# One attention-and-FFN block: head quads of the last two query tiles regrouped, VectorE's share of the exponentials chosen by new rules, and the first stage reordered

## The chip, the cores and the metric

The kernel runs on one core of a Trainium2 chip. The metric is the device time of one execution in microseconds (us), as the median of several runs. A NeuronCore has five engines with a queue each: TensorE (PE, matrix products into PSUM), ScalarE (ACT, here the exponentials), VectorE (DVE, elementwise work), GpSimd (POOL) and SyncE (SP, which issues nearly all DMAs here). PSUM has eight banks of 128 x 512 fp32 values.

## The reference, cut to what matters

```python
mod = (silu(c) @ w_mod)                      # six rows of 512: sa, ca, ga, sb, cb, gb
h = layernorm(x) * (1 + ca) + sa             # x is 2048 tokens x 512
qkv = h @ wqkv                               # 32 heads of 16
p = softmax(q k^T / 4)                       # 32 heads x 2048 x 2048
x = x + ga * ((p @ v) @ wo)
h = layernorm(x) * (1 + cb) + sb
x = x + gb * ((gelu(h @ w_gate) * (h @ w_up)) @ w_down)   # F = 1792
```

## The kernel before, in words

**Scores in banks.** The queries are cut into six sets (`SETS`, line 31): three of 512 tokens, one of 256, and the last two tiles of 128 tokens each (sets 4 and 5 in the code's numbers). Heads go in eight quads of four. A *unit* is a quad with a set; the first `QS = 5` quads (line 34) of the last two tiles are taken together, as units of 256 queries with the sets (4, 5), and the other three quads separately, first all of set 4, then all of set 5 (lines 1199 to 1201). A unit is cut into *rounds*: one round has four banks, one per head, each of 128 keys on the partitions by 512 columns (one key tile by 512 queries, two by 256 or four by 128). A unit of 512, 256 or 128 queries has 16, 8 or 4 rounds. There are 2048 banks in all, in one fixed sequence; `pos` is the place in it, and `ends[k]` the place where set k is complete: 512, 1024, 1536, 1792, 2000 and 2048. So the separate units lie at 1952 to 2000 (set 4) and 2000 to 2048 (set 5).

**The main loop** (`stream`, line 1192) puts three banks of scores (`CH`) into one half of a six-bank PSUM tile `ps_sc`, ACT takes their exponential in one instruction into a ring `E` of twelve banks, and PE multiplies them with the values into `ps_pv`, whose 17th row per head is the softmax's sum. While one half is on ACT, PE fills the other.

**Rounds on VectorE.** In some steps DVE takes one of the three banks instead of ACT: it writes an integer that, read as bf16, is close to the exponential (line 1394), and in four such steps a whole round. Four shifted copies of that round (`shift_task`, line 1472, `mreg<-dreg` or `mreg<-mreg` in the trace) with four scaled sets of values then average the error out; PE multiplies all five. Only rounds over the last four key tiles qualify: four of a 512-unit's rounds, two of a 256-unit's, one of a 128-unit's. A round is given (lines 1358 to 1374) when DVE is free within 700 ns by the planner's own clock, fewer than eight DVE steps wait (`BACK`), one of three buffers is free, the round lies less than 96 and at least `AHEAD = 24` banks ahead of `pos`, and, after `ends[2]`, the side work's credit is below `CREDIT = 1024`.

**Side work.** All other PE work (projections, output projection `side_wo`, FFN `side_ffn`) is a list of generators (`plan`, line 1118), taken strictly in order, with a bank `ps_mi` of its own. Each entry has a start and a due place in the sequence; `credit` grows by the columns left over the banks left, and PE does side work where credit and slack allow (lines 1350 and 1421). A generator that has to wait for something yields None (`until`, line 771), and `next_side` then returns None. The FFN of set 3 is due at `ends[4] - 20`, and what follows, the end of set 4, starts at `ends[4] - 16` (lines 1134 to 1143): the sums of its quads 6 and 7 (`near_end`, line 935: a product with `self32` spreads the sums, a reciprocal, and a product into `onorm`), its output projection, and then in `either` three things at once: the first two chunks of its FFN (`side_ffn(k, EARLY)`), the output projection of set 5 without its last quad (`wo_last`) and the rest of set 4's FFN (`tail_rest`). The last two wait for "last", when all scores are in PSUM. Quad 6 of set 5 gets its sums by a `near_end` behind the two chunks (line 1058). For the other quads the sums go through DRAM by small DMAs (`unit_end`, line 1494).

**DVE's and ACT's small work** is a list of tasks; `step` (line 1085) takes the first one that is ready, by `urgency` (line 1075). `tail` (line 1536) runs what is left when the last scores have been multiplied: sums of quad 7 of set 5, its output projection, LayerNorm, transposes, and the FFN of that tile, all in a row (`tail_end`, `tail_last`). All orders are settled when the program is built, by a cost model in the kernel's text; on the chip each engine runs its queue in order, with semaphores.

**First stage** (`prologue`, line 499). LayerNorm of the first four token tiles on DVE (tile 1 on ACT), two groups of 16 one-column products for the modulation (`mod_cols`, 4 to 7 and then 0 to 3, each from a 512 KB piece of `w_mod`), an addition `modA` on DVE, 16 transposes, `modulate`, the first projections and the first scores. `warm_up(n)` is n products of 128 x 512 on zeros.

Of the kernel before, what the change touches and what calls it, by code (L numbers as in the profile page):

```python
# [6 lines left out]
ALU = mybir.AluOpType  # L7
# [6 lines left out]
P = 128  # L14
# [16 lines left out]
SETS = ((0, 512), (512, 512), (1024, 512), (1536, 256), (1792, 128), (1920, 128))  # L31
OCOL = (0, 0, 0, 0, 256, 384)
BCOL = (0, 0, 0, 0, 0, 128)
QS = 5
CH = 3
SC = 2 * CH
NSL = 12
# [3 lines left out]
NK = 3  # L41
CREDIT = 1024
NS = 4
AHEAD = 24
FLOW = 3
URGENT = 9
LATE = 2
# [1 line left out]
BACK = 8  # L49
# [369 lines left out]
class _Kernel(_Recorder):  # L419
# [79 lines left out]
    def prologue(self):  # L499
# [46 lines left out]
        self.stt(self.sc_bf[:, :], self.tcol[:, :], 1.0, self.scp[:, 0, 0:NDC], ALU.add, ALU.mult)  # L546
        self.ln_stat(2)
        self.ln_stat(3)
        self.warm_up(7)
        self.mod_cols(self.scp[:, 1, 0:8], 0, range(4, 8))  # L550
        self.warm_up(3)
        self.mod_cols(self.scp[:, 1, 0:8], 0, range(4))
        self.warm_up(2)
        self.ln_rstd(0, 4)
        nb = self.nwt[:, 0:4]
        self.stt(nb, self.mv[:, 0:4, 0], -1.0, self.rstd[:, 0:4], ALU.mult, ALU.mult)
        for t in range(4):
            dst = self.tb1[:, 0, t, :]
            if t != 1:
                self.ln_norm(t, dst)  # L560
                if t == 0:
                    self.tt(dve, self.modA[:, :], self.modA[:, :], self.scp[:, 1, 0:8], ALU.add)
            else:
                self.act(dst, self.xs[:, t, :], ACT.Identity, bias=nb[:, t:t + 1], scale=self.rstd[:, t:t + 1])
        qb = [self.scp[:, 0, 0:256], self.scp[:, 1, 0:256]]
        kb = self.pv[:, 0:256]
        pts = []
# [202 lines left out]

    def until(self, key):
        while not self.dry and key not in self.have:
            yield None

    def side_first(self):
# [193 lines left out]
    def side_ffn(self, gi, part=None):  # L969

        q0, W = SETS[gi]
        n = W // P
        tiles = [q0 // P + i for i in range(n)]
        mi = self.mi[:, :]
        c0 = BCOL[gi]
        prod = self.prodT if W == 512 else self.prodL
        flow = gi < FLOW
        kpb = 512 // W
        chunks = []
        width = max(2, kpb)  # L980
        for a in range(0, NFC, width):
            chunks.append(range(a, min(NFC, a + width)))

        def load(x, ci):
            if flow and ci < len(chunks):
                v = (self.B_w_gate, self.B_w_up)[x].rearrange("(a p) n -> p a n", p=P)
                self.dma("sp", self.wst[x][ci % 2], v[:, :, 2 * P * ci:2 * P * ci + 2 * P], "st%d%d" % (x, ci % 2))

        def load_down(i):
            if flow:  # L990
                v = self.B_w_down.rearrange("(f p) n -> p f n", p=P)
                self.dma("sp", self.wdst[i], v[:, 2 * i:2 * i + 2, :], "sd%d" % i)

        yield from self.until(("ln2", gi))
        if flow:
            load(0, 0)
            load(1, 0)
        else:
            yield from self.until("weights")
        for h in range(2):  # L1000
            yield from self.side_t(lambda t: self.normed(gi, t), n, h,
                                   lambda dc: self.t2T[:, dc, c0:c0 + W], self.modB)

        def up(x, ci, sub):
            for s, fc in enumerate(sub):
                for dci in range(NDC):
                    if flow:
                        lhs = self.wst[x][ci % 2][:, dci, P * (fc % 2):P * (fc % 2) + P]
                    else:
                        lhs = self.up_w((self.wg, self.wu)[x], fc, dci)  # L1010
                    yield W, lambda s=s, lhs=lhs, dci=dci: self.mm(
                        mi[:, W * s:W * s + W], lhs, self.t2T[:, dci, c0:c0 + W], start=(dci == 0), stop=(dci == NDC - 1), whole=W == P)

        def G(ci):
            fcs = chunks[ci]
            m = len(fcs)
            g, w = self.gw[:, ci % 2, 0, 0:m * W], self.gw[:, ci % 2, 1, 0:m * W]
            load(0, ci + 1)
            for b0 in range(0, m, kpb):
                sub = fcs[b0:b0 + kpb]  # L1020
                yield from up(0, ci, sub)
                self.copy("dve", g[:, W * b0:W * (b0 + len(sub))], mi[:, 0:W * len(sub)])
                if b0 + kpb >= m and not self.dry:
                    self.task([lambda: self.tt("dve", w, g, g, ALU.mult),
                               lambda: self.ts("dve", w, w, GELU_C, 1.0, ALU.mult, ALU.add),
                               lambda: self.tt("dve", w, w, g, ALU.mult),
                               ("act", lambda: self.act(w, w, ACT.Tanh, scale=TANH_C0))], ("gelu", gi, ci))
                yield END

        def U(ci):  # L1030
            fcs = chunks[ci]
            m = len(fcs)
            g, w = self.gw[:, ci % 2, 0, 0:m * W], self.gw[:, ci % 2, 1, 0:m * W]
            yield from self.until(("gelu", gi, ci))
            load(1, ci + 1)
            for b0 in range(0, m, kpb):
                sub = fcs[b0:b0 + kpb]
                k = len(sub)
                yield from up(1, ci, sub)
                self.stt(w[:, W * b0:W * (b0 + k)], w[:, W * b0:W * (b0 + k)], 1.0, mi[:, 0:W * k], ALU.add, ALU.mult)  # L1040
                if b0 + kpb >= m:
                    self.tt("dve", prod[:, fcs[0]:fcs[0] + m, c0:c0 + W], w.rearrange("p (k n) -> p k n", k=m),
                            g.rearrange("p (k n) -> p k n", k=m), ALU.mult)
                yield END
        nch = len(chunks) if part is None else part
        for i in range(3):
            load_down(i)
        for ci in range(nch + 1):
            if ci < nch:
                yield from G(ci)  # L1050
                if ci >= nch - 2:
                    load_down(3 + ci - nch + 2)
            if ci >= 1:
                yield from U(ci - 1)
                if ci >= nch - 1:
                    load_down(5 + ci - nch + 1)
        if part is not None:
            yield from self.near_end(gi + 1, 6, self.mi[:, 0:P])
            if not self.dry:
                self.done(("part", gi))  # L1060
            return
        for i in range(n):
            for fc in range(NFC):
                yield 512, lambda i=i, fc=fc: self.mm(
                    mi, prod[:, fc, P * i:P * i + P], (self.wdst if flow else self.wd)[fc // 2][:, fc % 2, :], start=(fc == 0), stop=(fc == NFC - 1))
            self.down_fin(mi, tiles[i])
            yield END
        self.done(("ffn", gi))
# [5 lines left out]

    def urgency(self, tk):

        if tk[1] is not None and tk[1][0] == "shift" and self.plain[tk[1][1]] <= LATE:
            return -2
        if tk[1] is None or tk[1][0] in ("st2", "ln2", "den"):
            return -1  # L1080
        if tk[1] is None or tk[1][0] != "shift":
            return 1
        return 0 if self.plain[tk[1][1]] <= URGENT else 2
# [108 lines left out]
    def stream(self):  # L1192
        self.split = True
        self.tasks = []
        self.live = {}
        self.have = {("k", 0, 0), ("q", 0, 0), ("v", 0, 0)}
        self.credit = 0
        self.open = False
        units = [((k,), qd) + SETS[k] for k in range(4) for qd in range(8)]
# [3 lines left out]
        rounds = []  # L1203
# [15 lines left out]
        for u in units[2:]:  # L1219
# [3 lines left out]
            for r in plain[:m] + list(range(len(plain), n)) + plain[m:]:  # L1223
                add(u, r)
        nseq = len(seq)
        self.work = self.plan(ends, nsplit)
        self.slot = {}
        vec = set()
# [17 lines left out]
        quad = None  # L1246
# [84 lines left out]
        while cg <= group[units[-1]]:  # L1331
# [16 lines left out]
            if tq is not None and tq <= t + 30:  # L1348
# [7 lines left out]
                    continue  # L1356
                g = None
                if len(mem) == CH and "modB" in self.have and self.free["dve"] < t + 700:
                    while quad is None and cand and rounds[cand[0]][2] < pos + AHEAD:
                        cand.pop(0)  # L1360
                    overdue = {x[1][1] for x in self.tasks if x[1] is not None and x[1][0] == "shift" and self.plain[x[1][1]] <= LATE}
                    if quad is not None:
                        if not overdue - {quad["rnd"][0]}:
                            g = quad["rnd"][2] + quad["j"]
                    elif (not overdue and cand and self.quad_free and (pos < ends[2] or self.credit < CREDIT) and rounds[cand[0]][2] < pos + 96 and self.backlog() < BACK
                          and ("vs", rounds[cand[0]][0][1] // 2) in self.have
                          and all(k in self.have for k in self.keys(seq[rounds[cand[0]][2]]))):
                        rnd = rounds[cand.pop(0)]
                        quad = {"rnd": rnd, "j": 0, "k": self.quad_free.pop(0), "ready": [], "n": NS + 1, "slots": {}}
                        left[rnd[0]] += NS  # L1370
                        self.plain[rnd[0]] -= 1
                        g = rnd[2]
                        vec.update(range(g, g + 4))
                        mem, after = take(CH)
# [369 lines left out]
```

## Time and profile before

| what | before |
|---|---|
| median of 3 runs | 864.12 us (861.3 to 864.8) |
| the profiled execution, its own time | 864.73 us |
| its span, first to last instruction | 862.6 us (2.1 us lie around it) |
| busy: PE, DVE, ACT | 801.2, 694.8, 833.8 us |
| ACT's first and last exponential | starts 14.87, ends 841.08 us |
| ACT instructions of 1536 and 1024 columns on `E<-ps_sc` | 376 and 316 |
| DVE instructions that take a bank (192 `dreg<-ps_sc`, 96 `mreg<-ps_sc`) | 288, so 72 rounds |

Times in the profile are us from the span's start. A line of the timeline has start, duration, engine, source line, operation, `out<-in`, count, and in brackets the engine's idle time before it and what ended it. PE is engine work, PEld weight loads, a `q` after an engine's name its sequencer. Durations overlap for pipelined instructions.

### The profile page before, as it was taken

What the parts mean: (1) busy time and instruction counts of PE and PEld (TensorE: products, weight loads), DVE (VectorE), ACT (ScalarE), POOL (GpSimd) and SP (SyncE); (2) the same over time, 40 slices, a digit from 0 to 9 for tenths busy, and PEclk for the clock granted to TensorE, in tenths of its full rate; (3) what the DMA queues carried; (4) which work ended last, traced back from release to release, by engine and by line L of the source; (5) the groups of instructions that cost most, each with busy time, mean ns of one, the idle gap of its engine ahead of it and who ended that gap; (6) DMA issues with size and microseconds to landing.
All of it is one profiled execution on the core that took longest, in us unless ns stands there. A gap on an engine that the chain in (4) does not pass through costs nothing.

```text
span 862.6 us, 27597 instructions
## 1 busy us (share of the span) xinstructions
PE 801.2 (93%) x12436; PEld 286.5 (33%) x12436; DVE 694.8 (81%) x1340; ACT 833.8 (97%) x747; POOL 4.5 (1%) x12
## 2 busy tenths in 40 slices
PE   7889999999999899999999999999999889999988
PEld 3333332322222222222222222222343233354456
DVE  6865989978889989888988989989987763687255
ACT  6999999999999999999999999999999999999992
POOL 1000000000000000000000000000000000000000
PEclk9999999989999999999999999999999999999999
DMA  9000000000003121210002112120134231500000
GB/s 310 9 26 15 4 10 9 10 9 9 10 3 93 33 56 33 57 33 16 14 15 81 38 41 57 34 57 9 46 92 119 73 86 44 152 11 10 21 5 14
DMA packets 63807, 38.06 MB, mean 44 GB/s; under 512 B 17389, under 2 KB 61546, under 8 KB 63690
## 3 DMA queue, kind: packets, MB, share of 16 engines
q1 hardware_dynamic: 62632, 35.65, 14.6%
q8 instruction: 97, 1.59, 0.8%
q10 hardware_dynamic: 1058, 0.66, 0.3%
q14 instruction: 20, 0.16, 0.1%
HBM read 33.68 MB, written 2.61 MB: 42 GB/s over the span
## 4 chain that ended last, share of the span: by engine, by line
ACT 77%; PE 14%; DVE 6%; DMA 2%; issue 1%; SPq 0%; DVEq 0%
ACT E L326 74%; PE ps_sc L313 6%; PE ps_mi L313 5%; PE ps_pv L313 3%; ACT wreg L326 3%; DVE mreg L338 1%; DVE st L366 1%; DVE hreg L338 1%; DMA rb<-scr_rec 1%; DMA den<-scr_den 0%; DMA xs<-in_A_x_dram 0%; SPq L376 0%; DVE nwt L330 0%; DVE wreg L338 0%; DVE dreg L338 0%
## 5 line engine op out<-in xcount | busy, mean ns | idle before, releaser
L326 ACT ACTIVATE E<-ps_sc 128x1536 bf16<-128x1536 f32 (+2 forms) x698 | 806.0, 1340 | 13.0 <-PE ps_sc L313 12.7
L313 PE MATMUL ps_sc<-qT,kmo 32*128 32x512 bf16 (+2 forms) x1408 | 178.7, 323 | 11.3 <-ACT E L326 9.8
L313 PE MATMUL ps_sc<-qT,kme 32*128 32x512 bf16 (+2 forms) x1344 | 173.6, 333 | 13.1 <-ACT E L326 10.2
L313 PE MATMUL ps_pv<-E,vaug 128*17 128x512 bf16 (+2 forms) x2352 | 171.5, 323 | 2.3 <-DVE vaug L347 1.0
L338 DVE TENSOR_SCALAR dreg<-ps_sc 128x512 uint16<-128x512 f32 x192 | 132.3, 690 | 33.1 <-PE ps_sc L313 30.4
L338 DVE TENSOR_SCALAR mreg<-dreg 128x2048 uint16<-128x2048 uint16 x192 | 124.8, 681 | 0.4 <-PE ps_pv L313 0.4
L313 PE MATMUL ps_mi<-wreg,mreg 128*32 128x512 bf16 (+2 forms) x1504 | 110.4, 370 | 11.4 <-DVE wreg L343 6.6
L313 PE MATMUL ps_pv<-mreg,vs 128*17 128x512 bf16 (+2 forms) x1344 | 100.8, 350 | 1.5 <-DVE mreg L338 1.4
L313 PEld LDWEIGHTS ps_sc<-qT,kmo 32*128 32x128 bf16 x1408 | 48.2, 91 | 125.3 <-ACT E L326 96.8
L313 PEld LDWEIGHTS ps_sc<-qT,kme 32*128 32x128 bf16 x1344 | 45.5, 91 | 131.5 <-ACT E L326 96.3
L338 DVE TENSOR_SCALAR mreg<-ps_sc 128x512 uint16<-128x512 f32 x96 | 66.2, 690 | 19.5 <-PE ps_sc L313 17.6
L313 PEld LDWEIGHTS ps_pv<-E,vaug 128*17 128x17 bf16 x2352 | 52.4, 89 | 86.3 <-issue 60.9
L338 DVE TENSOR_SCALAR mreg<-mreg 128x2048 uint16<-128x2048 uint16 x96 | 63.0, 683 | 0.0
L313 PEld LDWEIGHTS ps_mi<-wreg,mreg 128*32 128x32 bf16 (+1 forms) x1504 | 34.0, 95 | 62.3 <-issue 20.6
L347 DVE CAST wreg<-ps_mi 128x512 bf16<-128x512 f32 x51 | 35.0, 686 | 15.4 <-PE ps_mi L313 14.6
L343 DVE SCALAR_TENSOR_TENSOR wreg<-wreg,ps_mi 128x512 bf16<-128x512 bf16 x51 | 34.9, 684 | 13.5 <-PE ps_mi L313 8.1
L313 PE MATMUL ps_mi<-hreg,wreg 128*32 128x512 bf16 (+1 forms) x496 | 40.2, 382 | 2.0 <-DVE hreg L338 1.0
L313 PEld LDWEIGHTS ps_pv<-mreg,vs 128*17 128x17 bf16 x1344 | 31.2, 89 | 31.2 <-DVE mreg L338 13.9
L313 PE MATMUL ps_mi<-wo,onorm 128*32 128x512 bf16 x480 | 37.8, 383 | 0.6 <-DVE xs L330 0.6
L330 DVE TENSOR_TENSOR wreg<-wreg 128x1024 bf16<-128x1024 bf16 (+1 forms) x60 | 35.6, 602 | 0.7
L313 PE MATMUL ps_mi<-mreg,hreg 128*32 128x512 bf16 x384 | 32.5, 384 | 0.0
L330 DVE TENSOR_TENSOR onorm<-osb,rb 128x512 bf16<-128x512 f32 (+2 forms) x43 | 23.4, 547 | 11.3 <-DMA rb<-scr_rec 11.2
(147 smaller groups left out, 574.0 us busy)
## 6 DMA issues: line engine op xcount, KB each, us to landing
mreg<-in_B_w_up_dram SPq DMA_DIRECT2D x25, 256.0 KB, 3.2
mreg<-in_B_w_gate_dram SPq DMA_DIRECT2D x21, 256.0 KB, 3.0
rb<-scr_rec SPq DMA_DIRECT2D x96, 32.0 KB, 1.8
mreg<-in_B_w_down_dram SPq DMA_DIRECT2D x12, 256.0 KB, 2.7
dreg<-in_B_w_down_dram SPq DMA_DIRECT2D x9, 256.0 KB, 4.0
mreg<-in_w_mod_dram SPq DMA_DIRECT2D x1, 2048.0 KB, 12.4
out_dram<-xs SPq DMA_DIRECT2D x15, 128.0 KB, 1.7
xs<-in_A_x_dram SPq DMA_DIRECT2D x3, 512.0 KB, 8.1
```

Source lines behind the costliest of these rows:

```text
L313: return self.rec("pe", lambda e: e.matmul(out, lhsT, rhs, start=start, stop=stop, tile_position=tp), [lhsT, rhs], [out], cost=(n, int(rhs ...
L326: return self.rec("act", lambda e: e.activation(out, in_, func, scale=scale, **kw), rd, wr, cost=self.cost("act", out, [in_], "act"))
L330: return self.rec(eng, lambda e: e.tensor_tensor(out, a, b, op), [a, b], [out], cost=self.cost(eng, out, [a, b], "tt"))
L338: return self.rec(eng, lambda e: e.tensor_scalar(out, a, s1, s2, **kw), rd, [out], cost=self.cost(eng, out, [a], "ts") + (60 if len(rd) > ...
L343: return self.rec("dve", lambda e: e.scalar_tensor_tensor(out, a, s, b, op0=op0, op1=op1), rd, [out], cost=self.cost("dve", out, [a, b], " ...
L347: return self.rec(eng, lambda e: e.tensor_copy(out, in_), [in_], [out], cost=self.cost(eng, out, [in_], "ts"))
L366: return self.rec("dve", lambda e: e.bn_stats(out, in_), [in_], [out], cost=self.cost("dve", out, [in_], "bn"))
```

## The change

1. `QS` goes from 5 to 4: quad 4 of the last two tiles is computed as two units of 128 queries instead of one of 256. The number of banks stays. The separate units lie at 1920 to 1984 and 1984 to 2048, and `ends[4]` is 1984 instead of 2000; the due places that hang on it move with it.
2. `AHEAD` becomes (30, 44), and it is no longer the round but the end of its unit that must lie so far ahead: 44 banks for units of 512 queries, 30 for the others.
3. After `ends[2]` a round may also be given to VectorE at high credit when the side work is waiting and what it last asked for is an "onorm" or "osb" (a quad's normalised output, or its sums).
4. Quad 6 of set 5 gets its `near_end` between two chunks of set 4's FFN, as soon as its sums are there; else behind them as before.
5. Tasks "rec", "onorm", "stats", "rstd" and set 5's "ln2" go ahead of all others on DVE.
6. First stage: `warm_up` 7, 3, 2 becomes 11, 1, 0, and the `modA` addition goes behind the last LayerNorm product.

```diff
-QS = 5
+QS = 4
-AHEAD = 24
+AHEAD = (30, 44)
 # prologue
-        self.warm_up(7)
+        self.warm_up(11)
         self.mod_cols(self.scp[:, 1, 0:8], 0, range(4, 8))
-        self.warm_up(3)
+        self.warm_up(1)
         self.mod_cols(self.scp[:, 1, 0:8], 0, range(4))
-        self.warm_up(2)
         self.ln_rstd(0, 4)
...
                 self.ln_norm(t, dst)
-                if t == 0:
-                    self.tt(dve, self.modA[:, :], self.modA[:, :], self.scp[:, 1, 0:8], ALU.add)
             else:
                 self.act(dst, self.xs[:, t, :], ACT.Identity, bias=nb[:, t:t + 1], scale=self.rstd[:, t:t + 1])
+        self.tt(dve, self.modA[:, :], self.modA[:, :], self.scp[:, 1, 0:8], ALU.add)
 # until
         while not self.dry and key not in self.have:
+            self.waiting = key
             yield None
 # side_ffn
+        early = [part is not None]
+
+        def near():
+            if early[0] and ("osb", gi + 1, 6) in self.have:
+                early[0] = False
+                yield from self.near_end(gi + 1, 6, self.mi[:, 0:P])
...
         for ci in range(nch + 1):
+            yield from near()
             if ci < nch:
                 yield from G(ci)
+                yield from near()
...
         if part is not None:
-            yield from self.near_end(gi + 1, 6, self.mi[:, 0:P])
+            if early[0]:
+                yield from self.near_end(gi + 1, 6, self.mi[:, 0:P])
 # urgency
+        if tk[1] is not None and tk[1][0] in ("rec", "onorm", "stats", "rstd") or tk[1] in ((("ln2", len(SETS) - 1, h) for h in range(2))):
+            return -3
 # stream
+        self.waiting = "",
+        last = {u: g0 + 4 for u, r, g0 in rounds}
-                    while quad is None and cand and rounds[cand[0]][2] < pos + AHEAD:
+                    while quad is None and cand and last[rounds[cand[0]][0]] < pos + AHEAD[rounds[cand[0]][0][3] == 512]:
                         cand.pop(0)
...
-                    elif (not overdue and cand and self.quad_free and (pos < ends[2] or self.credit < CREDIT) and rounds[cand[0]][2] < pos + 96 and self.backlog() < BACK
+                    elif (not overdue and cand and self.quad_free and (pos < ends[2] or self.credit < CREDIT or (self.next_side() is None and self.waiting[0] in ("onorm", "osb"))) and rounds[cand[0]][2] < pos + 96 and self.backlog() < BACK
```

## The prediction

> **What bounds the kernel now.** I read the page's chain first, then ACT's groups by form, then timelines of the first 16 us and of the end.
>
> ```profile
> L326 ACT ACTIVATE E<-ps_sc 128x1536 bf16<-128x1536 f32 x376 | 535.8, 1540 | 2.4 <-PE ps_sc L313 2.3
> L326 ACT ACTIVATE E<-ps_sc 128x1024 bf16<-128x1024 f32 x316 | 319.6, 1117 | 2.4 <-PE ps_sc L313 2.3
> ...
> 811.66 24.37 ACT L326 ACTIVATE E<-ps_sc 128x1536 bf16<-128x1536 f32 x18
> ```
>
> The page's chain is ACT 77%, PE 14%, DVE 6%, and nearly all of ACT's part is the exponentials of line 326. ACT idles 2.4 us in front of each of the two forms, out of 826 us between its first and last one (14.87 to 841.08). So the time is four pieces: 14.9 us before the first exponential, a stream that ACT alone sets, 21.5 us from the last one to the span's end (862.6 - 841.1), and 2.1 us around the span. The last row gives a step of three banks: (24.37 - 1.54) / 17 = 1.34 us, or 0.45 us a bank. The two forms differ by 1540 - 1117 = 423 ns, so **a round given to DVE saves four times that, 1.69 us**, as long as DVE keeps up.
>
> **First stage (edit 6).** Timeline:
>
> ```profile
> 8.27 1.44 PE L313 MATMUL ps_mi<-dreg 128*128 128x512 bf16 x3
> 9.50 0.61 PE L313 MATMUL ps_sc<-sc_bf,mreg 128*128 128x1 bf16 x16
> 9.97 1.01 PE L313 MATMUL ps_mi<-dreg 128*128 128x512 bf16 x2
> 10.15 0.16 DVE L330 TENSOR_TENSOR modA<-modA,ps_sc 128x8 f32<-128x8 f32 x1 [1.58 <-PE ps_sc L313]
> 10.78 1.06 PE L317 MATMUL ps_sc<-ident,dreg 128*128 128x128 bf16 x10
> 11.71 1.69 DVE L338 TENSOR_SCALAR hreg<-ps_sc,modA 128x256 bf16<-128x256 bf16 x5 [0.75 <-PE ps_sc L317]
> ```
>
> Three warm-ups stand between the two groups of column products and two behind them, and DVE stops 1.58 us at the `modA` addition with two LayerNorm products queued behind it. After the change one warm-up stands between. The first group ends at about 8.24; the second needs the 512 KB piece of `w_mod` that SP issues at 1.81 and that takes 6.8 us to land (DMA issues), so it starts at 8.65 instead of 9.50, and PE is free at 9.07 instead of 10.78. DVE's three products run from 8.16 without the stop and end at about 9.2, ACT's tile 1 ends at 9.09. The addition now waits behind these products, until about 9.25, and `modulate` is behind it. Eight transposes from 9.07 plus their latency (0.67 us at 56 ns each, 1.06 at 107 ns, both spacings in this trace) put the first `modulate` at 9.75 to 10.1 instead of 11.71. The weights of the first projections have landed by then (issued 1.84, 7.5 us). Gain 1.6 to 2.0, **taken 1.8**. The four warm-ups put ahead fill PE's gap from 5.8 to 7.85, where it waits for DVE and for data; they cost nothing. Nothing later has a fixed time: the stream shifts as a whole.
>
> The clock belongs to this:
>
> ```profile
> 4.57:7.99 3.42, 1.40 (x12) 0.57 (x11) 2.88 (x12) 1.02 (x4) 0.58 (x1) 1.00 1.07 321
> 7.99:11.40 3.41, 3.41 (x43) 2.03 (x41) 1.35 (x6) 0.81 (x1) 0.00 (x0) 0.51 1.14 317
> ```
>
> After a stretch with PE busy 1.40 of 3.42 us (first figure) the granted clock (third from the end) was 0.51 in the next; the four warm-ups bring that to about 2.3. The stretch after 7.99 was full and was followed by 1.00 (12.00:14.00). In the changed kernel it holds two groups of column products, one warm-up, 16 transposes and some nine projections. The Trainium skill ("TensorE: Matmul & The Clock Gate", Part 4) says of transposes that they don't count as PE-busy the same way; by that rule this stretch might count as idle and the projections and first scores would run at half clock. The trace can't settle it, since its transposes stand among warm-ups. I make it a rival.
>
> **Four and four (edit 1).** The work stays: rows of scores and values take 0.39 and 0.40 us for 256-query units (x6, x8 at 788) and 0.40 and 0.40 for 128-query units (x12, x16 at 801). One more unit ends through DRAM: seven more SP DMAs (SP's queue is mostly empty) and one more reciprocal and product on DVE. What moves: set 4 is complete 16 banks earlier, 16 x 0.45 = 7.2 us. Its quad sums now stand at 812.9 and 820.0 (`osb<-ps_pv`), its output projection runs at 822.1 to 825.4, its statistics at 826.1, and its two FFN chunks end at 841.1, with the last exponential. The side work ahead of it, set 3's FFN, ends at 811.6; it isn't held by credit but by PE and by DVE's gelu chain, so an earlier due place hardly moves it. So set 4's end runs about 6 us earlier: quad 7's sums at 812.8, just after that FFN.
>
> Against it: PE prefers side work to scores when credit is high, and an earlier due place raises credit. The one long ACT gap of the stream's last 60 us is of that kind, 0.95 us at 808.99 `<-PE ps_sc`. I add 0.3 us (0 to 1.5).
>
> **Rounds (edits 2 and 3).** In the middle (280 to 600) 395 DVE instructions on `dreg` and `mreg` at eight a round make 49 rounds, and DVE is busy 36 of 40 us: it limits the count, not the candidates. For 512-unit rounds the new bound is the old one for the last round of four (unit start + 20) and later for the first three; it changes which round is taken, not how many: 0, with -1 to +1. Nearer bounds free buffers sooner but leave less time: 30 banks are 13.4 us, and a round needs four evacuations of 690 and four copies of 680 ns, 5.5 us of DVE.
> After `ends[2]` credit rules. The windows of DVE's work on `mreg`:
>
> ```profile
> 280.00:600.00 320.00, 128.19 (x196) 1.00 0.14 39
> ...
> 780.00:812.00 32.00, 5.34 (x8) 1.00 0.06 12
> 812.00:841.00 29.00, 0.00 (x0) 1.00 0.05 10
> ```
>
> One round was given in 780 to 812 and none later, while DVE was busy 14.6 of the last 29 us and PE ran fillers (`ps_sc<-xs,ident`). Edit 3 opens this stretch when side work stands at an "osb" or "onorm". In the kernel before it would: from 811.6 to 813 and 814.8 to 820. In the changed one quad 7's sums come 7.2 us earlier, and the wait is only as long as set 3's FFN ends ahead of 812.8. The round at 780 delays that FFN (its four `mreg<-mreg` copies stand at 786.1 to 789.2, and PE waits for gelu there); higher credit makes it unlikely to be given, and then the FFN ends some 4 us earlier and the wait fits one or two rounds. So from -1 to +4 net; **I take +1, 1.7 us**, the middle of the likely 0 to 2.
>
> **Tail (edits 1, 4, 5).** DVE's timeline behind the last exponential:
>
> ```profile
> 842.14 0.95 DVE L350 RECIPROCAL rb<-ps_mi 128x128 f32<-128x128 f32 x1
> 843.00 0.90 DVE L350 RECIPROCAL rb<-ps_sc 128x128 f32<-128x128 f32 x1
> 843.81 0.42 DVE L330 TENSOR_TENSOR onorm<-osb,rb 128x128 bf16<-128x128 f32 x2
> ...
> 845.73 0.18 DVE L369 BATCH_NORM_AGGREGATE mv<-st 128x2 f32<-128x6 f32 x1
> 845.83 0.67 DVE L343 SCALAR_TENSOR_TENSOR hreg<-ps_sc,E 128x512 bf16<-128x512 f32 x1
> 846.42 0.14 DVE L338 TENSOR_SCALAR nwx<-mv 128x1 f32<-128x1 f32 x1
> ```
>
> Two quads' sums end side by side. Quad 6's came at 835.6 but waited for the FFN chunks; taken earlier (edit 4) its reciprocal, product and output product (0.21 us on PE) leave the path: 0.1 + 0.15 + 0.2 = 0.45. The 0.67 us product of set 4's FFN stands between aggregate and `nwx`; with edit 5 `nwx` follows at 845.95 instead of 846.42: 0.47. Set 4's remaining FFN starts earlier, since the chunks no longer fill PE to 840: its two products among the last tile's (849.3, 849.9; 0.22 us each) go, 0.4. Then PE is late next: from 849.7 to 859.2 it multiplies almost without a gap, and that stays. **Taken 1.3** (0 to 2).
>
> **Sum**, against the profiled execution: 864.73 - 1.8 - 1.3 - 1.7 + 0.3 = 860.2. It stands 0.6 above the median of 864.12, so the forecast for the median is **859.6 us**.
>
> **Rivals.**
> - *No round more, or one less* (edit 3 doesn't do what it says: set 3's FFN still ends after quad 7's sums, and the wait that it asks for is not there): 861.3, at -1 863.0. For it: 811.6 against 812.8. Chance 0.30.
> - *Two to four net*: 857.9 to 854.5. For it: DVE and PE idle in the last 29 us. Chance 0.24.
> - *The clock falls in the first stage*: the 12 projections (109 ns apart from 12.4 on) and the first scores double, about 1 us lost: 860.6. Chance 0.06.
> - *DVE's queue holds a bank* (slower than before). In the timeline a product waits for its sums from DRAM with all DVE work behind it:
>
> ```profile
> 819.74 0.29 DVE L330 TENSOR_TENSOR onorm<-osb,rb 128x128 bf16<-128x128 f32 x1 [4.70 <-DMA rb<-scr_rec]
> ```
>
> It costs nothing today, since no bank waits for DVE there. Given rounds in this stretch put evacuations behind it, and ACT stops when its other half is done: 4.70 - 1.34 = 3.4 us each. One such wait gives 863.0, two 866.4, three 869.8; from two on the kernel is slower than before. Against it: DVE's place in the order is planned, and the other five waits of that kind sum to 6.5 us. Chance 0.07.
>
> The forecast has 0.33. The range, 855.0 to 864.0, takes in the first two rivals nearly whole and the clock. Half a per cent is 4.3 us, about what a measurement of this kernel tells from no change: faster by more (under 859.8) has a bit over half of the forecast, the second rival and some of an unforeseen gain at the end, 0.47; within it 0.46; slower 0.07.
>
> **What would show it.** First exponential near 13.1. ACT's 1024-column instructions: 316 + 4 a round, with DVE's bank evacuations 288 + 4 a round; windows on `mreg` and `dreg` after 800 say where. Set 4's statistics about 6 us earlier, measured from the last exponential. Last exponential to the span's end near 20.2. Long gaps of ACT `<-DVE` or `<-PE` after 780 would show the last rival or the PE price; a clock of 0.5 near 12 us the third. The forecast is wrong first of all if the count of rounds moves by more than two.

## The result, and the profile after

| | before | after |
|---|---|---|
| median (5 runs each) | 864.02 us (861.3 to 864.8) | 859.09 us (858.58 to 861.82) |
| the profiled execution, its span | 864.73, 862.6 us | 860.08, 858.3 us |
| mean granted clock of the profiled execution | 0.994 | 1.000 |
| first exponential starts, last one ends | 14.87, 841.08 | 14.15, 836.34 |
| ACT idle between the two | 4.86 us | 2.86 us |
| last exponential to the span's end | 21.55 us | 22.00 us |
| rounds on DVE | 72 | 73 |

The ratio is 0.9958 [0.9938, 0.9977]: 0.42% faster; the interval lies clear of 1, but the difference is far below the 2% from which a change counts as faster here. The forecast was 859.6. Its sum for the profiled execution was 860.2 and that execution took 860.08. The total came out; of its terms, only the round did.

The page's chain stays an ACT chain (74%; PE 16%). The groups by form give the round:

```profile
L326 ACT ACTIVATE E<-ps_sc 128x1536 bf16<-128x1536 f32 x372 | 530.7, 1540 | 1.7 <-PE ps_sc L313 1.2
L326 ACT ACTIVATE E<-ps_sc 128x1024 bf16<-128x1024 f32 x320 | 323.8, 1120 | 1.4 <-PE ps_sc L313 1.2
```

Four instructions went from 1536 to 1024 columns: one round more. The windows of the work on `mreg` tell where (DVE's evacuations and copies are the third busy figure, behind the stretch's length, PE and its weight loads):

```profile
780.00:812.00 32.00, 1.06 (x32) 0.77 (x32) 2.77 (x4) 1.00 0.08 17
812.00:841.00 29.00, 5.19 (x176) 3.89 (x176) 5.19 (x8) 1.00 0.05 6
```

The prediction shows the windows of DVE alone before: eight instructions on `mreg` in the first stretch, none in the second. The round near 780 is gone and two stand behind 807, one with its four banks in `mreg` from 807.33 and one in `dreg` from 811.03. Set 3's FFN ended at 804.4 instead of 811.6, and until quad 7's sums at 811.6 the side work waited. That is the wait that edit 3 asks for, and two rounds fit it, as the prediction had it.

The time between the two profiled executions is -4.65 us: first exponential -0.72; stream -4.02 (one round -1.69; ACT's gaps -2.00; the rest, 0.33, is other work of ACT); tail +0.44; around the span -0.35.

**The first stage.** Timeline of the kernel after:

```profile
9.38 0.54 PE L313 MATMUL ps_sc<-sc_bf,mreg 128*128 128x1 bf16 x16 [2.23 <-DMA mreg<-in_w_mod_dram]
9.79 0.38 PE L313 MATMUL ps_mi<-dreg 128*128 128x512 bf16 x1
10.00 0.54 PE L313 MATMUL ps_sc<-sc_bf,mreg 128*128 128x1 bf16 x16
10.40 0.72 PE L317 MATMUL ps_sc<-ident,dreg 128*128 128x128 bf16 x10
```

The order is the one forecast, and DVE's `modA` addition no longer holds products. But in this execution the two pieces of `w_mod` landed at 9.25 and 9.83 us, against 7.71 and 8.62 before, so PE stood 2.23 us in front of the first group. The landing isn't the kernel's doing: in E5, the same kernel again, the second piece lands at 8.57, and over the twelve profiles below, issued at the same time, between 8.2 and 9.4 us.

**The gaps.** Of ACT's 2.00 us, 1.30 are three gaps at 180 to 184 that of these two profiles only the one before has. Windows of the kernel before, all engines; the third figure from the end is the granted clock, the first busy figure PE's:

```profile
175.25:178.66 3.41, 2.52 (x28) 0.55 (x29) 2.28 (x4) 3.41 (x4) 0.00 (x0) 1.00 0.03 5
178.66:182.07 3.41, 3.41 (x27) 0.61 (x30) 2.13 (x4) 2.58 (x4) 0.00 (x0) 0.51 0.00 0
182.07:185.49 3.42, 3.42 (x33) 0.57 (x27) 1.43 (x4) 2.94 (x3) 0.00 (x0) 0.50 0.13 26
```

For two windows the clock is at half, after one in which PE was busy 74% of the time. The clock's steps, at 8.06, 11.47, 178.72 and 185.55, lie on one grid of 3.413 us ((178.72 - 8.06) / 3.413 = 50.0). The Trainium skill ("TensorE: Matmul & The Clock Gate", Part 1) states such a free-running window of 3413 ns; the trace agrees. The change has no edit there, and other runs of the changed kernel have lower clocks too (0.998 in one of its five): the loss goes with where the grid falls in a run, and it was in the number that I predicted from. The profiles of all runs bear this out: in the five with this fall (before, E1, E3, E4, E8) a window of the grid starts 160.4 to 160.7 us behind the first exponential, in the eight without it at 158.7 to 159.7 or at 161.3 (E7, whose load there is changed, aside). That the 74% alone bring the fall is not so: in the same execution PE is busy 67% from 284.54 to 287.95, in the changed kernel 54% from 660.94 to 664.35, both windows of the grid, and the clock stays at 1.00 behind them. The other gap that went is the 0.95 us at 808.99: set 3's FFN, which stood in front of the scores there, had ended at 804.4.

**The tail.** Timeline behind the last exponential (836.34), PE and DVE:

```profile
836.37 0.90 PE L313 MATMUL ps_mi<-wreg,mreg 128*128 128x128 bf16 x13
837.20 0.62 PE L313 MATMUL ps_pv<-E,vaug 128*17 128x128 bf16 x32
837.75 0.34 PE L313 MATMUL ps_mi<-wreg,mreg 128*128 128x128 bf16 x3
837.88 0.29 DVE L347 COPY osb<-ps_pv 128x128 f32<-128x128 f32 x1 [1.51 <-PE ps_pv L313]
838.13 0.69 DVE L343 SCALAR_TENSOR_TENSOR wreg<-wreg,ps_mi 128x512 bf16<-128x512 bf16 x1
...
838.86 0.43 DVE L330 TENSOR_TENSOR hreg<-wreg 128x512 bf16<-128x512 bf16 x1
839.20 0.95 DVE L350 RECIPROCAL rb<-ps_sc 128x128 f32<-128x128 f32 x1
```

Set 4's second FFN chunk, which ended with the last exponential before, now ends behind it. Its 13 products stand in PE's queue ahead of the last 32 products with the values, and its two DVE products ahead of quad 7's reciprocal. The aggregate of set 5 comes 5.56 us behind the last exponential, against 4.65. Edit 5 works (`nwx`, the next step of set 5's LayerNorm, 0.22 us behind the aggregate instead of 0.69), and edit 4 works (quad 6's reciprocal at 835.06, ahead of the last exponential). Set 4's statistics come 16.94 us ahead of the last exponential's end instead of 14.95: 2.0 us earlier, not the 6 forecast. Why set 4 is late although its units end 16 banks earlier, the same timeline shows, DVE only:

```profile
811.64 0.28 DVE L347 COPY osb<-ps_pv 128x128 f32<-128x128 f32 x1
...
813.06 1.35 DVE L338 TENSOR_SCALAR dreg<-ps_sc 128x512 uint16<-128x512 f32 x2 [0.42 <-PE ps_sc L313]
814.33 0.95 DVE L350 RECIPROCAL rb<-ps_mi 128x128 f32<-128x128 f32 x1
...
815.54 2.49 DVE L338 TENSOR_SCALAR mreg<-mreg 128x2048 uint16<-128x2048 uint16 x4
818.52 0.69 DVE L330 TENSOR_TENSOR xs<-xs,ps_mi 128x512 bf16<-128x512 bf16 x1 [0.50 <-PE ps_mi L313]
...
820.49 0.69 DVE L338 TENSOR_SCALAR mreg<-dreg 128x2048 uint16<-128x2048 uint16 x1
...
823.87 0.41 DVE L338 TENSOR_SCALAR hreg<-xs,mv,rstd 128x512 bf16<-128x512 bf16 x1
```

From quad 7's sums (811.64) to `hreg` it is 12.2 us here and 8.1 in E2 below, which has no late rounds. Of the difference 1.5 us stand in front of the reciprocal, which has two evacuations of the second round ahead of it, 0.8 between it and set 4's addition, and 1.7 between the aggregate and `hreg`, where four copies of the second round stand one by one between the steps of the LayerNorm. The first round's copies stand in front of the addition too, but it waits for PE behind them (0.50 in the brackets).

### The profile page after: what moved, and what is told of

The parts are those of the page before. It is cut to its first block, busy times and chain, and to the rows that moved or that the text cites. A ratio compares the mean times of both kernels' runs of the same rounds, so it can differ in the third digit from the quotient of the medians.

```text
span 858.3 us, 27911 instructions
## 1 busy us (share of the span) xinstructions
PE 797.3 (93%) x12580; PEld 288.0 (34%) x12582; DVE 700.3 (82%) x1351; ACT 831.8 (97%) x747; POOL 4.5 (1%) x12
## 4 chain that ended last, share of the span: by engine, by line
ACT 74%; PE 16%; DVE 7%; DMA 1%; issue 1%; SPq 0%; ACTq 0%; DVEq 0%
ACT E L326 72%; PE ps_mi L313 6%; PE ps_sc L313 6%; PE ps_pv L313 3%; ACT wreg L326 2%; DVE mreg L338 1%; DMA mreg<-in_w_mod_dram 1%; DVE st L366 1%; DVE wreg L343 1%; DVE hreg L338 1%; DVE wreg L347 1%; SPq L376 0%; DVE dreg L338 0%; DVE nwt L330 0%; DMA rb<-scr_rec 0%
## 5 line engine op out<-in xcount | busy, mean ns | idle before, releaser
L338 DVE TENSOR_SCALAR dreg<-ps_sc 128x512 uint16<-128x512 f32 x196 | 135.1, 690 | 35.0 <-PE ps_sc L313 32.6
L338 DVE TENSOR_SCALAR mreg<-dreg 128x2048 uint16<-128x2048 uint16 x196 | 127.8, 681 | 0.4 <-PE ps_pv L313 0.4
L313 PE MATMUL ps_mi<-wreg,mreg 128*32 128x512 bf16 (+2 forms) x1504 | 110.2, 370 | 13.2 <-DVE wreg L343 6.8
L313 PE MATMUL ps_pv<-mreg,vs 128*17 128x512 bf16 (+2 forms) x1408 | 102.8, 344 | 2.1 <-DVE mreg L338 1.8
L313 PEld LDWEIGHTS ps_sc<-qT,kme 32*128 32x128 bf16 x1408 | 47.5, 91 | 130.5 <-ACT E L326 97.4
```

Of the source, the lines that this page charges most:

```text
L313: return self.rec("pe", lambda e: e.matmul(out, lhsT, rhs, start=start, stop=stop, tile_position=tp), [lhsT, rhs], [out], cost=(n, int(rhs ...
L338: return self.rec(eng, lambda e: e.tensor_scalar(out, a, s1, s2, **kw), rd, [out], cost=self.cost(eng, out, [a], "ts") + (60 if len(rd) > ...
```

## The experiments

Each was run beside the kernel before. Each expectation was written before its run and names a theory A and a rival B; the text behind it says which held. Since the clock differs from run to run, I give two numbers: the ratio of medians, and the difference at equal clock, from one least-squares fit over all 231 runs (time = kernel + chip + slope x lost clock). The slope is 0.62 us for each 0.001 of mean clock, the scatter 0.88 us. At equal clock the changed kernel is 2.4 us (1.7 to 3.1) faster than before; a mean clock of 1.000 was granted in 35 of 96 runs of the kernel before, and in 9 of 14 of the changed one; that these shares differ by more than chance is not shown.

**E1, the first stage alone** (before with edit 6).

> The kernel before with the reordered first stage alone (edit 6). Theory A (what the two traces say: the stage now waits for the 512 KB pieces of w_mod, which landed at 9.3 and 9.8 us in the trace after and at 7.7 and 8.6 in the trace before): first exponential at 13.1 when they land early and 14.2 when late, time 862.3 to 863.4, 72 rounds on VectorE. Rival B (the first stage with its clock is nearly the whole gain): 859 to 860.

862.94 us, ratio 0.9993 [0.9977, 1.0009], at equal clock -0.3 (+-0.6). Its first exponential stands at 12.99, close to the 13.1 that I forecast, and the time hardly moves: theory A.

**E2, without the wait rule** (after without edit 3, 71 rounds).

(Of the line, only the condition that changes is shown.)

```diff
-(pos < ends[2] or self.credit < CREDIT or (self.next_side() is None and self.waiting[0] in ("onorm", "osb")))
+(pos < ends[2] or self.credit < CREDIT)
```

> The changed kernel without edit 3, the rule for rounds at waits for sums: 71 rounds instead of 73. Theory A (two rounds save 3.4 us on ACT, but their copies on DVE push set 4's LayerNorm and its two FFN chunks behind the last exponential, where they cost about 1.8 us): ACT ends 3.4 us later, the tail from the last exponential is 20.2 instead of 21.9 us, 860.7 us. Rival B (rounds pay in full, the tail does not depend on them): 862.5 us with a tail of 21.9.

863.9 us, 1.0006 [0.9996, 1.0017], at equal clock +0.6. Two rounds are gone, 3.4 us by the price of a round and 3.0 (+-0.9) measured. Theory A fails and rival B is near (862.5 us with a tail of 21.9; the profiled execution, at a clock of 1.000, took 862.68): the tail is 22.21 instead of 20.2, although set 4's aggregate stands at 816.6, 22.0 us ahead of the last exponential's end (838.67). Here it is other side work that stands in front:

```profile
837.61 1.68 PE L313 MATMUL ps_sc<-wo,onorm 128*32 128x512 bf16 x28
838.69 1.28 ACT L326 ACT_TABLE_LOAD   x1
839.12 0.84 PE L313 MATMUL ps_sc<-wreg,qT 128*32 128x128 bf16 x48
839.79 0.62 PE L313 MATMUL ps_pv<-E,vaug 128*17 128x128 bf16 x32
```

What "last" frees (the output projection of set 5, the rest of set 4's FFN) goes ahead of the last products with the values, and these start 1.1 us behind the last exponential.

**E3, five shared quads** (after with `QS = 5`, 75 rounds).

> The changed kernel with five shared quads (edit 1 undone, all other edits kept): 75 rounds, since the wait for the sums lies inside the separate units. Theory A: ACT ends 3.4 us earlier than in the changed kernel, but all of set 4's LayerNorm and FFN falls behind the last exponential, tail 24 to 27 us, 859 to 862 us. Rival B (rounds pay in full): 855.7 us.

862.17 us, 0.9988 [0.9974, 1.0002], at equal clock -0.1. The stream is the shortest of all (819.8 us) and the tail the longest (29.7, beyond the 24 to 27 of theory A, whose mechanism it is): set 4's aggregate comes at 831.1, 1.8 us ahead of the last exponential's end, and its whole FFN is behind it. Two rounds more than in the changed kernel are paid back twice.

**E4, four and four alone** (before with `QS = 4`, 71 rounds).

> The kernel before with four shared quads alone (edit 1): 71 rounds, one less than before. Theory A: ACT ends 1.7 us later, set 4's two FFN chunks end well before the last exponential, and the tail is 20 to 20.7 instead of 21.5 us: 864.5 to 865.5 against 864.0. Rival B (the regrouping by itself brings the gain): 861 or less.

863.89 us, 1.001 [0.9998, 1.0023], at equal clock +1.0. Theory A holds for the round and fails for the tail (20 to 20.7 expected); rival B's gain is not there. The parts: one round fewer (+1.7), tail 22.2 by the same order of PE's queue as in E2 (+0.65), and the gap at 808 shrinks from 0.95 to 0.18 us.

**E5, the changed kernel again**, beside E6 to E8.

> The changed kernel as it is, with more runs beside the kernel before. In its five runs so far four had a mean granted clock of 1.000 and one 0.998, while 24 of 35 runs of the kernel before had less than 1. Theory A: the pause of the clock near 180 us (half rate for 6.8 us in the profiled run before, three ACT gaps of 1.3 us in sum) strikes by the phase of the run, in any of these kernels; then the changed kernel too has it in a third to two thirds of its runs, its median is 859 to 861, and runs of equal clock differ from those of the kernel before by 2.8 us (859.05 against 861.85 where the clock is 1.000). Rival B: the new order of the first stage keeps the clock up at 180 us; then nearly all runs show 1.000 and the median stays at 859.1.

859.39 us (859.0 to 862.26), 0.9959 [0.9941, 0.9977]. Four of nine runs have less than 1.000, so theory A holds against rival B, under which nearly all would have it. That the change has no part at all in the share is not shown. First exponential at 12.98, gaps 3.19, tail 22.00.

**E6, values first.**

```diff
+            if ok[0] and pos >= nseq:
+                pv_do(tp[0])
+                continue
             if ok[0] and (ok[1] or self.pe_mode == 2 or ...
```

(The last line is cut.)

> The changed kernel with one rule more: once all scores are in PSUM, the last products with the values go ahead of side work on PE. Theory A: the 0.45 us that the tail grew by is PE's order: 13 products of set 4's FFN (0.90 us) stand between the last exponential and the last 32 products with the values, so the copy of quad 7's sums comes 1.54 us behind the last exponential, against 0.85 before. Then here that copy comes 0.7 us sooner, set 5's aggregate 0.5 to 0.8 us sooner, and the time is 0.4 to 0.8 us lower than the changed kernel's, with 73 rounds. Rival B: what is late is set 4's FFN itself, whose two DVE products (0.69 and 0.43 us) stand in front of the reciprocal; then the copy comes sooner but the aggregate stays within 0.2 us and so does the time.

858.97 us, 0.9945 [0.9926, 0.9964], at equal clock 0.1 under the changed kernel: no difference. Rival B. Timeline of DVE, the last exponential ends at 835.04:

```profile
835.80 0.29 DVE L347 COPY osb<-ps_pv 128x128 f32<-128x128 f32 x1 [0.73 <-PE ps_pv L313]
836.89 0.69 DVE L343 SCALAR_TENSOR_TENSOR wreg<-wreg,ps_mi 128x512 bf16<-128x512 bf16 x1 [0.80 <-PE ps_mi L313]
837.62 0.43 DVE L330 TENSOR_TENSOR hreg<-wreg 128x512 bf16<-128x512 bf16 x1
837.96 0.95 DVE L350 RECIPROCAL rb<-ps_sc 128x128 f32<-128x128 f32 x1
```

The copy comes 0.76 us behind the last exponential instead of 1.54, and then the reciprocal waits in the queue behind set 4's two products, as long as before.

**E7, values first, filled near 176 us.**

```diff
-        return FILL - w
+        return (6400 if 384 <= self.at < 412 else FILL) - w
```

(`self.at` is set to `pos` in the main loop.)

> The kernel of the run before with five more filler products on PE near 176 us (a higher aim for PE's columns in banks 384 to 411), where PE was busy about half of a microsecond in every trace and the clock fell to a half some 1 to 2 us later in four of six traces. Theory A: the clock falls there because PE is too little busy over one window of about 3.4 us; then nearly all runs show a mean clock of 1.000, the ACT gaps near 180 us (1.3 us) are absent, and the median is 1 to 2 us under that of the same kernel without the fillers wherever that one has the pause in half of its runs. Rival B: the fall has another cause; then the share of runs with a lower clock stays at a third or more and the fillers change nothing or cost 0.2 us each.

860.22 us, 0.9977 [0.9956, 0.9999], at equal clock 0.9 slower than E6; 5 of 12 runs below 1.000. Theory A fails in its result: in the profiled run the loss of clock isn't gone but sits further on, and three windows long instead of two (183.34 to 193.58).

```profile
180.00:184.00 4.00, 3.14 (x32) 0.92 0.02 2
184.00:188.00 4.00, 4.00 (x25) 0.50 0.11 37
188.00:192.00 4.00, 3.85 (x30) 0.50 0.00 2
```

Again it follows a window that is not full, but other windows that are not full pass with the clock at 1.00 behind them. What load keeps the clock up stays open.

**E8, the old first stage** (after without edit 6).

> The changed kernel with the old first stage (edit 6 undone), 73 rounds. Theory A: edit 6 is worth little where the clock holds in the first stage: the first exponential followed the landing of the second piece of the modulation's weights by 4.7 us with the old stage (13.71 after 9.04) and by 4.2 to 4.9 us with the new one, so here the time is that of the changed kernel within 0.5 us at equal clock, and only runs in which the clock halves in the first stage, as in the profiled run before (first exponential 6.2 us after the landing), are 1.5 us longer. Rival B: edit 6 brings its 1.8 us in every run; then this kernel is 1.8 us slower than the changed one, 860.9 at a clock of 1.000.

860.21 us, 0.9963 [0.9948, 0.9979], at equal clock 0.3 slower than the changed kernel (+-0.8): theory A. Its six runs at 1.000 have a median of 859.06, the changed kernel's five in that call 859.37. Its profiled execution starts its first exponential at 14.79 and E4's, with the same old stage, at 13.71. PE of E4, then of E8:

```profile
8.48 0.81 PE L313 MATMUL ps_mi<-dreg 128*128 128x512 bf16 x3
9.13 0.54 PE L313 MATMUL ps_sc<-sc_bf,mreg 128*128 128x1 bf16 x16
9.75 0.38 PE L313 MATMUL ps_mi<-dreg 128*128 128x512 bf16 x1
9.96 0.72 PE L317 MATMUL ps_sc<-ident,dreg 128*128 128x128 bf16 x10
```

```profile
8.26 1.44 PE L313 MATMUL ps_mi<-dreg 128*128 128x512 bf16 x3
9.50 0.61 PE L313 MATMUL ps_sc<-sc_bf,mreg 128*128 128x1 bf16 x16
9.97 1.01 PE L313 MATMUL ps_mi<-dreg 128*128 128x512 bf16 x2
10.78 0.98 PE L317 MATMUL ps_sc<-ident,dreg 128*128 128x128 bf16 x10
```

Three warm-ups take 0.81 us at full clock and 1.44 at half. The old stage costs 1.1 us more in an execution whose clock halves there, and my base was one.

**E9, copies held**, and **E10, held and values first**.

```diff
+HOLD = "st2", "ln2"
...
     def step(self, eng, t):
+        hold = any(tk[1] is not None and tk[1][0] in HOLD and tk[1][1] in (len(SETS) - 2, SETS[len(SETS) - 2][0] // P) and (tk[2] is None or tk[2]()) for tk in self.tasks)
         for tk in sorted(self.tasks, key=self.urgency):
+            if hold and eng == "dve" and tk[1] is not None and tk[1][0] == "shift":
+                continue
```

(E10 adds the three lines of E6.)

> The changed kernel in which DVE makes no shifted copies (the copies of a given round) while set 4's statistics and LayerNorm can run; still 73 rounds. Theory A: set 4's end is late because the eight copies of the two late rounds (2.49 and 2.7 us) stand in front of its addition and between the steps of its LayerNorm (hreg at 823.87, 12.5 us before the last exponential; 20 us before it in the kernel with 71 rounds). Then with the copies between the steps gone set 4's LayerNorm ends about 2.5 us earlier, its two FFN products leave the stretch behind the last exponential, but PE's side work still stands in front of the last products with the values, as it did with 71 rounds, so the tail stays at 21.5 to 22.2 us and the time at 859.0 to 859.6. Rival B: the order of DVE's queue is all; then the tail falls to 21 us and the time by 1 us.

> Both rules together: no copies while set 4's LayerNorm can run, and the last products with the values ahead of side work. Theory A: either alone leaves the other in the way (values first alone moved the copy of quad 7's sums from 1.54 to 0.76 us behind the last exponential and the aggregate not at all, 5.56 to 5.62). Together the reciprocal follows the copy at once, 1.5 to 1.7 us behind the last exponential instead of 2.9, the aggregate stands at 4.3 to 4.7 instead of 5.6, and the tail is 20.9 to 21.3; the time is about 1 us under that of the changed kernel, near 858.2 at a clock of 1.000. Rival B: PE's work behind the last exponential (18.5 us of 22.0) sets the end; what DVE gains waits at PE, the tail stays above 21.7 and the time within 0.3 us.

E9: 861.91 us, 0.9979 [0.9964, 0.9994]; at equal clock 2.1 slower than the changed kernel. E10: 861.39 us, 0.998 [0.9963, 0.9998]; 0.8 slower. In the tail theory A holds in both: set 4's `hreg` comes 1.8 us after the aggregate in E9 (820.96 after 819.20) instead of 3.75; the tail is 22.21 in E9 and 21.06 in E10, where the copy stands 0.66, the reciprocal 1.54 and the aggregate 4.16 us behind the last exponential. Neither theory had what it costs. Timeline of E10 (its lines are numbered one higher):

```profile
833.34 0.62 PE L314 MATMUL ps_pv<-mreg,vs 128*17 128x128 bf16 x32
834.51 0.28 DVE L348 COPY osb<-ps_pv 128x128 f32<-128x128 f32 x1
834.85 0.49 PE L314 MATMUL ps_mi<-osb,self 128*128 128x128 f32 x2 [0.89 <-DVE osb L348]
835.26 0.40 PE L314 MATMUL ps_pv<-E,vaug 128*17 128x128 bf16 x16
835.60 0.62 PE L314 MATMUL ps_sc<-qT,kmo 32*128 32x128 bf16 x24
836.04 2.79 ACT L327 ACTIVATE E<-ps_sc 128x1536 bf16<-128x1536 f32 x2 [1.85 <-PE ps_sc L314]
```

With the copies held, the round's products with the values stand later in PE's queue (833.34, which is 820.0 behind the first exponential, against 831.07 or 816.9 in the changed kernel), so quad 6's sums are copied out late (834.51); edit 4's spreading product is already in PE's queue and waits for them, the scores stand behind it, and ACT stops 1.85 us. E9 has the same stop (1.85 us at 834.42), the changed kernel and E6 have none. The 0.94 us won in E10's tail is given back twice over in the stream.

**E11, without edits 4 and 5.**

> The changed kernel without edits 4 and 5 (quad 6's sums wait for the FFN chunks again, the last tile's DVE tasks have no precedence), 73 rounds. Theory A: the two are worth what the prediction said, 0.45 and 0.47 us, and hid a loss of 1.3 us in the same tail; then the tail is 22.5 to 23.0 us and the time 0.5 to 1 us above the changed kernel. Rival B: with PE's side work and set 4's products ahead of quad 7 anyway, they bring nothing; the tail stays at 22.0 to 22.2 and the time within 0.3 us.

864.68 us, 1.0029 [1.001, 1.0049]. Both theories missed by far: the tail is 27.21, 5.2 us longer. DVE and PE, the last exponential ends at 835.79:

```profile
839.85 1.06 PE L313 MATMUL ps_mi<-wreg,mreg 128*128 128x128 bf16 x16
...
841.84 0.38 PE L313 MATMUL ps_mi<-osb,self 128*128 128x128 f32 x2
...
842.26 0.96 DVE L350 RECIPROCAL rb<-ps_mi 128x128 f32<-128x128 f32 x1 [0.18 <-PE ps_mi L313]
...
845.15 0.18 DVE L369 BATCH_NORM_AGGREGATE mv<-st 128x2 f32<-128x6 f32 x1
```

Quad 6's sums wait for both FFN chunks, and with the late rounds these end 6 us behind the last exponential. Measured from the last exponential, the aggregate is 3.8 us later than in the changed kernel. PE then has 0.32 us of work between 845 and 848, and its clock is 0.54 from 848 to 851, where PE is busy throughout: that can make up most of the other 1.4 us, but no run takes it apart. No run of this kernel has a mean clock of 1.000, so its loss of clock is at least in part its own, and the number at equal clock (3.1 over the changed kernel) leaves it out.

**E12, the old bound** (edit 2 undone).

> The changed kernel with the old bound for rounds (edit 2 undone: the round, not its unit's end, lies 24 banks ahead), 73 rounds. Theory A: as the prediction said, the bound changes which round is taken and not how many; the time is that of the changed kernel within 0.4 us at equal clock. Rival B: with the nearer or farther bound a buffer or a copy is late somewhere; then ACT shows new gaps of 0.5 us or more and the time differs by over 0.8 us.

861.93 us, 0.9981 [0.9962, 1.0], at equal clock the same as the changed kernel to 0.1 us, with the same 73 rounds and the same tail (22.00). Its profiled execution has some new gaps (0.64 at 761, 0.52 at 835). Only three of its twelve runs had a clock of 1.000, which makes its median. At equal clock theory A holds, though the gaps that rival B named are there in this one execution.

## Why the prediction was right in sum, by its steps

- *First stage, -1.8: wrong in size.* The first exponential did move to 13.0 to 13.2 where the weights landed as early as before (E1, E2, E5, E6), and -1.9 is what the two profiles of before and E1 show. But the base, the profiled execution before, had its clock at half from 8.06 to 11.47. With a full clock the old stage starts its first exponential at 13.71 (E4, second piece landed at 9.04), the new one at 13.32 (E10, 9.11): 0.4. E1 and E8 both measure 0.3 at equal clock, no more than their error. I had shown the half clock in my own fence and taken it for part of the kernel. That half clock stands in two of the three profiles with the old stage and in none of the eleven with the new one, so part of the 1.8 may come as executions that lose no clock there; the fit books this under the clock, and so few profiles settle no share. In the profiled execution after, late weights left -0.72.
- *The clock as a rival (transposes that might not keep it up): did not happen.* The stretch with 16 transposes was followed by a clock of 1.00 in every profile of the new stage. Whether transposes count as PE-busy in the same way, which by the Trainium skill ("TensorE: Matmul & The Clock Gate", Part 4) they don't, no run here decides, since the stretch also held projections.
- *Four and four: the early FFN was right, its price wrong.* Set 3's FFN ended at 804.4, 7 us earlier where I wrote some 4. I priced PE's preference for side work at +0.3; instead the 0.95 us gap at 808 went.
- *Rounds, +1 net: right*, by the mechanism named: the round near 780 not given (E4 shows that the regrouping alone takes it away; that credit is the reason is argued), two in the wait. E2 takes the two away and loses 3.0 us.
- *Tail, -1.3: wrong, +0.44.* The parts that I counted are there (quad 6's reciprocal, `nwx`). What failed is the sentence that set 4's remaining FFN starts earlier. Alone, four and four does bring set 4 forward (its statistics come 22.3 us ahead of the last exponential's end in E4 and 22.8 in E2, against 15.0), but PE's queue then puts work freed by "last" in front of the last values: +0.65. With the two rounds the last exponential itself comes 3.4 us earlier, and their evacuations and copies hold set 4's reciprocal and LayerNorm. I costed a round at DVE's evacuations and copies as time that DVE had idle, and did not ask which step of set 4 stands behind them. And edits 4 and 5, which I costed against the kernel before at 0.92, are worth 5.2 in the tail with the two rounds in (E11; 3.1 at equal clock).
- *What made up for it:* two terms short by 1.1 (first stage) and 1.75 us (tail) against ACT's gaps, 1.30 by the clock and 0.95 at 808, other work of ACT (0.33) and the time around the span (0.35). That the sum came out to 0.1 us was luck, by cancellation. So was part of the median: of the 4.9 us between the two medians, 2.4 stand at equal clock, and the rest is most likely the clock that these few executions were granted, which no term of the forecast had. The mechanisms account for a gain of 2.4 at equal clock: one round 1.69, the gap at 808 0.95, the first stage 0.3, the tail -0.45, in sum 2.5.
- *DVE's queue holding a bank: did not happen*; the longest ACT gap behind 780 in the kernel after is under 0.1 us.

Neither edit 6 nor edit 1 pays alone (E1 and E4 lie within 0.1% of before; the others were not run alone), and taking away edit 1 (E3), edit 3 (E2) or edits 4 and 5 (E11) from the whole each loses at least 2.3 us at equal clock. No kernel here is faster than the changed one by more than its error; E6 equals it.

## What to carry to other kernels

Work that is given to an idle engine late in a program must be priced by what stands behind it in that engine's queue, not by the engine's idle time: the two late rounds bought 3.4 us in the stream and would have cost 5 in the tail without edits 4 and 5 (E4's tail of 22.2 us against E11's of 27.2). Before pricing a stage from one profile, look whether its clock was granted there; compare edits at equal clock when the effect is below half a per cent, unless the edit itself costs clock, as in E11. And an order that only closes a gap in one queue (values first, copies held) moves the wait to the next instruction that stands in another.

## What was not expected of the hardware

- The landing of the same 512 KB transfer, issued at 1.8 us with the same traffic, varies from 8.2 to 9.8 us between executions and shifts the first exponential with it.
- PE's clock fell to half for two windows of 3.41 us in the middle of the program after a window with PE busy 74%, in the profiled executions of before, E1, E3, E4 and E8 at 177 to 179 us. Windows with PE busy 54 and 67% elsewhere were not followed by one. In the changed kernel PE stood idle for 2.23 us at 7.15 us without any fall, and in E11 0.32 us of work in 3 was followed by one. Which load over which window decides is not settled.
- Runs of one kernel differ with their mean granted clock: medians of 861.85 at 1.000, 863.3 at 0.998 and 865.3 at 0.996 for the kernel before on one chip.
